# Attention with beacon keys and a multiplicative feed-forward: from stages set by a scheduler to one hand-ordered stream

## The chip, the core and the metric

The kernel runs on one core of one Trainium2 chip. The metric is device time in microseconds. Engines are TensorE (PE; its weight loads are PEld), VectorE (DVE), ScalarE (ACT), GpSimd (POOL) and SyncE (SP). Each has its own instruction queue and works through it in order; semaphores join them. DMAs are issued from the SP or the POOL queue.

## What is computed

```python
B, H, S, Nb, D = (8, 8, 576, 16, 64)          # tokens: B*S = 4608
k_all = np.concatenate([beacon_k, k], axis=2)  # 592 keys
v_all = np.concatenate([beacon_v, v], axis=2)
scores = np.matmul(q, k_all.transpose(0, 1, 3, 2)) / np.sqrt(D)
# causal on the 576 own keys; the 16 beacon keys are always seen
a = np.exp(scores - scores.max(-1, keepdims=True))
a /= a.sum(-1, keepdims=True) + 1e-09
x = np.matmul(a, v_all)                        # -> [4608, 512]
return ((x @ w1) * (x @ w2) @ w3) @ w_out      # d_model 512, d_ff 1024
```

Inputs and output are f32 in DRAM. Both kernels work in f16 with f32 sums in PSUM.

## The kernel before

It is written stage by stage, and a scheduler orders the instructions from their dependences and from the number of buffers of each pool.

*Weights* (L85 to L114): each is loaded in f32, cast on DVE, and w3 is written back to DRAM in f16 (`w3s`) and read through eight DMA transposes (`w3T`). 64 matmuls then form `Wt` = w3 @ w_out, so that feed-forward needs only `Wt`.

*A batch* (loop over 8): q, k and v tiles are loaded in f32 (L168, SP), cast on ACT (q, k) or POOL (v) at L170, and q and k are written to DRAM in f16 (`qs`, `ks`, L201 and L205, POOL queue). For each of the four head pairs `t`, two DMA transposes bring q and k back with the head dimension on partitions (`qpT`, `kpT`, L215 and L216).

*Attention of a head pair*: scores are computed keys by queries, key tile after key tile (5 of them), into one PSUM tile `Ps` (L233, L238), exponentiated by ACT into `pT` (L243), and the diagonal block is masked by DVE (L253). Then v is stationary and `pT` moves: `P1` gets values (L265), `PD` gets denominators by a second stream with a tile of ones as weights (L272). A reciprocal of the whole `PD` (L281) and a product (L282) give `xT`, already transposed for feed-forward.

*Feed-forward* (`moe_chunk`, 512 tokens): 64 matmuls into `pab` (L135), scaled by ACT (`a_sb`) and multiplied by DVE (`gT`), then 32 into `po` (L148), scaled by ACT (`ot`) and stored. `pab` and `po` use the PSUM banks of `P1`, `PD` and `Ps`, one buffer each, so attention and feed-forward take turns. Chunk b − 1 is written ahead of batch b's attention; the last two chunks stand behind everything.

Of the kernel before, what the change touches and what calls it, by code (L numbers as in the profile page):

```python
# [19 lines left out]
def kernel(  # L20
# [24 lines left out]
    HD = H * D  # L45

    SC = 5
# [1 line left out]
    KJ = [min(P, NJ - jt * P) for jt in range(NJT)]
    SLO = [max(0, P * jt - Nb) for jt in range(NJT)]  # L50
# [2 lines left out]
    dramp = ctx.enter_context(tc.tile_pool(name="dram", bufs=1, space=bass.MemoryType.DRAM))

    xT = const.tile([P, NKT, M], FP16)
    w12 = const.tile([P, NKT, 2 * DF], FP16)
    Wt = const.tile([P, NFT, DM], FP16)
    ones = const.tile([P, 64], FP16)
    nc.vector.memset(ones, 1.0)
    ebias = const.tile([P, 1], FP32)  # L60
    nc.vector.memset(ebias, EXP_BIAS)
    LT = const.tile([P, P], FP16)
    LT0 = const.tile([P, 112], FP16)
    nc.vector.memset(LT, 1.0)
    nc.vector.memset(LT0, 1.0)
    for m, base in ((LT, 0), (LT0, Nb)):
# [10 lines left out]
    qs = dramp.tile([B, SC * P, NT, P], FP16)  # L77
    ks = dramp.tile([B, NJT * P, NT, P], FP16)
    w3s = dramp.tile([DF, DF], FP16)

    with (
        tc.tile_pool(name="wst", bufs=1) as wst,
        tc.tile_pool(name="wpsum", bufs=2, space=bass.MemoryType.PSUM) as wpsum,
    ):
        w12_32 = wst.tile([P, NKT, DF], FP32)  # L85
        for i, w in enumerate((moe_w1, moe_w2)):
            nc.sync.dma_start(w12_32, w.rearrange("(t p) f -> p t f", p=P))
            nc.vector.tensor_copy(
                w12[:, :, ds(i * DF, DF)],
                w12_32,  # L90
            )
        wo32 = wst.tile([P, NFT, DM], FP32)
        wo16 = wst.tile([P, NFT, DM], FP16)
        nc.sync.dma_start(wo32, moe_w_out.rearrange("(t p) n -> p t n", p=P))
        nc.vector.tensor_copy(wo16, wo32)
        w3_32 = wst.tile([P, NFT, DF], FP32)
        w3h = wst.tile([P, NFT, DF], FP16)
        w3T = wst.tile([P, NFT, DF], FP16)
        nc.sync.dma_start(w3_32, moe_w3.rearrange("(t p) r -> p t r", p=P))
        nc.vector.tensor_copy(w3h, w3_32)  # L100
        nc.sync.dma_start(w3s.rearrange("(t p) r -> p t r", p=P), w3h)
        for rt in range(NFT):
            nc.sync.dma_start_transpose(w3T[:, rt, :], w3s[:, ts(rt, P)])  # L103
# [21 lines left out]
    scale = float(D**-0.5)

    def moe_chunk(mc):
        gT = mp.tile([P, NFT, 512], FP16, tag="gT", name="gT")
        for kf in range(NFT):
            pab = aps.tile(  # L130
                [P, 2, 512], FP32, tag="P1" if kf % 2 == 0 else "PD", name="pab"
            )
            for i in range(2):
                for kt in range(NKT):
                    nc.tensor.matmul(  # L135
                        pab[:, i, :],
                        w12[:, kt, ds(i * DF + kf * P, P)],
                        xT[:, kt, ds(mc * 512, 512)],
                        start=(kt == 0),
                        stop=(kt == NKT - 1),  # L140
                    )
            a_sb = mp.tile([P, 512], FP32, tag="a_sb", name="a_sb")
            nc.scalar.activation(a_sb, pab[:, 0, :], AF.Copy, scale=GS)  # L143
            nc.vector.tensor_tensor(gT[:, kf, :], pab[:, 1, :], a_sb, ALU.mult)  # L144
        po = aps.tile([P, 4, DM], FP32, tag="Ps", name="po")
        for mt in range(4):
            for kf in range(NFT):
                nc.tensor.matmul(  # L148
                    po[:, mt, :],
                    gT[:, kf, ts(mt, P)],  # L150
                    Wt[:, kf, :],
                    start=(kf == 0),
                    stop=(kf == NFT - 1),
                )
# [163 lines left out]
```

## Time and profile before

| | |
|---|---|
| median of 3 runs | 668.42 us (667.52 to 668.67) |
| span of the profiled execution | 666.6 us, 7292 instructions |
| TensorE busy | 425.0 us, 64% |
| DVE, ACT, POOL busy | 256.4, 243.0, 64.9 us |
| first feed-forward weight matmul, first score matmul | 45.75 us, 91.11 us |
| DMA | 72.58 MB, 109 GB/s on average |

Busy time is the time in which an engine had an instruction at work; matmuls are pipelined, so a busy TensorE is not a full one. The granted clock is the share of full speed that TensorE was given; its two levels are 1.2 and 2.4 GHz. The chain follows the work that ended last back from the end, at each step to what released it.

### The profile page before, as it was taken

What the parts mean: (1) busy time and instruction counts of PE and PEld (TensorE: products, weight loads), DVE (VectorE), ACT (ScalarE), POOL (GpSimd) and SP (SyncE); (2) the same over time, 40 slices, a digit from 0 to 9 for tenths busy, and PEclk for the clock granted to TensorE, in tenths of its full rate; (3) what the DMA queues carried; (4) which work ended last, traced back from release to release, by engine and by line L of the source; (5) the groups of instructions that cost most, each with busy time, mean ns of one, the idle gap of its engine ahead of it and who ended that gap; (6) DMA issues with size and microseconds to landing.
All of it is one profiled execution on the core that took longest, in us unless ns stands there. A gap on an engine that the chain in (4) does not pass through costs nothing.

```text
span 666.6 us, 7292 instructions
## 1 busy us (share of the span) xinstructions
PE 425.0 (64%) x2848; PEld 201.7 (30%) x2848; DVE 256.4 (38%) x464; ACT 243.0 (36%) x357; POOL 64.9 (10%) x114
## 2 busy tenths in 40 slices
PE   0019116677667865785678666966696759665994
PEld 0003003333323333333333233323333323333441
DVE  2300004741464146424642455235532553255320
ACT  0002416534653464345434431344234323442331
POOL 0000110203002110210021001000100000000001
PEclk9999755589556965796659655965697569765998
DMA  8772879595939756662266111021001000100011
GB/s 340 290 201 50 215 165 243 107 247 153 265 98 212 213 133 156 149 190 50 37 147 192 49 37 19 18 65 37 19 16 48 1 0 17 47 1 1 16 48 63
DMA packets 172723, 72.58 MB, mean 109 GB/s; under 512 B 163856, under 2 KB 163984, under 8 KB 172688
## 3 DMA queue, kind: packets, MB, share of 16 engines
q1 hardware_dynamic: 166864, 53.10, 33.9%
q0 software_dynamic: 5824, 19.01, 7.4%
q8 instruction: 22, 0.36, 0.2%
q14 instruction: 13, 0.11, 0.1%
HBM read 39.32 MB, written 21.10 MB: 91 GB/s over the span
## 4 chain that ended last, share of the span: by engine, by line
PE 55%; ACT 19%; DMA 9%; DVE 8%; SPq 4%; issue 3%; POOL 0%; POOLq 0%; ACTq 0%
PE pab L135 21%; ACT pT L243 15%; PE po L148 9%; PE Ps L233 9%; PE P L265 7%; DVE rdb L281 6%; PE PD L272 6%; DMA w<-in_moe_w_dram 4%; ACT ot L156 3%; PE pw L107 2%; DMA t_k<-in_k_dram 2%; PE Ps L238 2%; SPq L103 1%; SPq L216 1%; DMA w3s<-w3h 1%
## 5 line engine op out<-in xcount | busy, mean ns | idle before, releaser
L243 ACT ACTIVATE pT<-Ps,ebias 128x1152 f16<-128x1152 f32 (+4 forms) x160 | 130.2, 814 | 143.9 <-PE Ps L238 137.3
L233 PE MATMUL Ps<-qpT,kpT 64*128 64x512 f16 (+4 forms) x320 | 77.1, 378 | 135.9 <-ACT pT L243 107.7
L135 PE MATMUL pab<-xT,w 128*128 128x512 f16 x576 | 143.5, 413 | 31.2 <-DVE rdb L281 30.8
L281 DVE RECIPROCAL rdb<-PD 128x576 f16<-128x576 f32 x32 | 120.2, 3757 | 65.9 <-PE P L265 37.8
L253 DVE TENSOR_TENSOR pT<-pT,LT 128x128 f16<-128x128 f16 (+2 forms) x320 | 55.3, 216 | 199.5 <-ACT pT L243 199.5
L265 PE MATMUL P<-pT,v 128*64 128x64 f16 (+6 forms) x640 | 113.3, 333 | 1.5 <-DVE xT L282 0.9
L272 PE MATMUL PD<-pT,ones 128*64 128x64 f16 (+6 forms) x640 | 107.3, 330 | 0.2 <-DVE pT L253 0.2
L135 PEld LDWEIGHTS <-w 128*128 128x128 f16 x576 | 60.2, 104 | 110.5 <-issue 54.1
L144 DVE TENSOR_TENSOR gT<-pab,a_sb 128x512 f16<-128x512 f32 x72 | 49.8, 691 | 105.5 <-ACT a_sb L143 105.5
L143 ACT ACTIVATE a_sb<-pab 128x512 f32<-128x512 f32 x72 | 43.0, 597 | 109.6 <-PE pab L135 109.2
L148 PE MATMUL po<-Wt,gT 128*128 128x512 f16 x288 | 69.2, 379 | 16.7 <-ACT ot L156 16.4
L265 PEld LDWEIGHTS <-v 128*64 128x64 f16 (+1 forms) x640 | 59.7, 152 | 37.0 <-issue 28.8
L272 PEld LDWEIGHTS <-ones 128*64 128x64 f16 (+1 forms) x640 | 63.5, 156 | 8.5 <-issue 1.9
L238 PEld LDWEIGHTS <-kpT 64*128 64x128 f16 (+1 forms) x320 | 22.4, 117 | 132.3 <-issue 130.8
L107 PE MATMUL pw<-wo,w3T 128*128 128x512 f16 x64 | 20.7, 476 | 48.2 <-DMA w3T<-w3s 47.9
L238 PE MATMUL Ps<-qpT,kpT 64*128 64x64 f16 (+1 forms) x320 | 48.7, 245 | 0.0
L233 PEld LDWEIGHTS <-kpT 64*128 64x128 f16 (+1 forms) x320 | 31.1, 114 | 49.6 <-issue 44.6
L156 ACT ACTIVATE ot<-po 128x512 f32<-128x512 f32 x36 | 21.5, 597 | 63.4 <-PE po L148 63.4
L148 PEld LDWEIGHTS <-gT 128*128 128x128 f16 x288 | 27.4, 97 | 56.4 <-issue 23.2
L157 POOL DMA_DIRECT2D out_dram<-ot x36 | 19.5, 543 | 231.3 <-ACT ot L156 231.3
L170 POOL CAST v<-t_v 128x512 f16<-128x512 f32 (+1 forms) x40 | 23.2, 615 | 138.4 <-PE PD L272 135.5
L170 ACT CAST q<-t_q 128x512 f16<-128x512 f32 (+1 forms) x40 | 24.2, 612 | 31.2 <-DMA t_q<-in_q_dram 31.1
(21 smaller groups left out, 94.3 us busy)
## 6 DMA issues: line engine op xcount, KB each, us to landing
out_dram<-ot POOLq DMA_DIRECT2D x36, 256.0 KB, 2.3
t_q<-in_q_dram SPq DMA_DIRECT2D x32, 256.0 KB, 3.7
t_k<-in_k_dram SPq DMA_DIRECT2D x24, 256.0 KB, 4.1
t_v<-in_v_dram SPq DMA_DIRECT2D x24, 256.0 KB, 4.2
w<-in_moe_w_dram SPq DMA_DIRECT2D x2, 2048.0 KB, 8.5
w<-in_moe_w_dram SPq DMA_DIRECT2D x1, 4096.0 KB, 19.1
qs<-q POOLq DMA_DIRECT2D x8, 512.0 KB, 4.6
ks<-k POOLq DMA_DIRECT2D x8, 512.0 KB, 4.2
```

Of the source, the lines that this page charges most:

```text
L135: nc.tensor.matmul(pab[:, i, :], w12[:, kt, ds(i * DF + kf * P, P)], xT[:, kt, ds(mc * 512, 512)], start=(kt == 0), stop=(kt == NKT - 1),)
L143: nc.scalar.activation(a_sb, pab[:, 0, :], AF.Copy, scale=GS)
L144: nc.vector.tensor_tensor(gT[:, kf, :], pab[:, 1, :], a_sb, ALU.mult)
L148: nc.tensor.matmul(po[:, mt, :], gT[:, kf, ts(mt, P)], Wt[:, kf, :], start=(kf == 0), stop=(kf == NFT - 1),)
L170: (eng.copy if eng is nc.scalar else eng.tensor_copy)(d16[:n, c], t32[:n])
L233: nc.tensor.matmul(Ps[:kj, hh, ds(lo, 512 - lo)], lhs, qpT[ds(hh * 64, 64), ds(lo, 512 - lo)],)
L238: nc.tensor.matmul(Ps[:kj, hh, ds(512, 64)], lhs, qpT[ds(hh * 64, 64), ds(512, 64)],)
L243: nc.scalar.activation(pT[:kj, :, jt, ds(lo, S - lo)], Ps[:kj, :, ds(lo, S - lo)], AF.Exp, bias=ebias[:kj], scale=scale,)
L253: nc.vector.tensor_tensor(pT[:kj, hh, jt, ds(lo, w)], pT[:kj, hh, jt, ds(lo, w)], msk[:kj, :w], ALU.mult,)
L265: nc.tensor.matmul(P1[ds(64 * hh, 64), ds(s0, sn)], v16[:kj, jt, ds(hh * 64 + 128 * t, 64)], pT[:kj, hh, jt, ds(s0, sn)], start=first, sto ...
L272: nc.tensor.matmul(PD[ds(64 * (1 - hh), 64), ds(s0, sn)], ones[:kj, 0:64], pT[:kj, 1 - hh, jt, ds(s0, sn)], start=first, stop=last,)
L281: nc.vector.reciprocal(rdb, PD)
```

## The change

The kernel is written anew for the same computation.

- *Loads* go from f32 in DRAM to f16 in SBUF in one casting DMA each, issued by POOL; the casts on DVE, ACT and POOL, and the DRAM copies `qs`, `ks`, `w3s`, are gone. Batches 0 and 1 and all weights are queued at the start, in the order q/k of 0, v of 0, w1, w2, batch 1, w3, w_out.
- *Transposes* of q, k and w3 read SBUF and write SBUF. w3 lies for the time in the second half of `xT`.
- *Scores* of a head pair are cut into four groups of 368, 512, 384 and 400 columns for each head (`GROUPS`, with `GO` their places in `pT`). `ps` has two buffers of two banks. The heads alternate matmul by matmul. There is one exponential a group, and one mask multiply for groups 0, 2 and 3.
- *Values*: a 128 x 128 block of probabilities is stationary, and 65 columns of `va` move: 64 of v and one of ones, so the denominator is column 64 of the same result (`BLK`, `DONE`). Queries now lie on partitions: the reciprocal is of 2 or 4 numbers a partition, and the product writes `x16`, [queries, 512].
- `x16` needs a transpose: for the last head pair of a batch five more DMA transposes write `xT`.
- *Feed-forward* has three PSUM banks of its own (`psM`) and is a Python generator that gives one matmul at a time. The output is scaled by DVE and stored from SP.
- *Order*: manual. Step s issues the scores of s + 2, some feed-forward matmuls, the mask of s + 1 and the values of s. There are 8 x 4 x 4 = 128 steps; feed-forward begins at step 20, and 696 of its 928 matmuls (with the 64 of `Wt`) lie between steps. Loads of batch b + 1 are issued in steps 0 to 4 of batch b, its transposes in steps 4 to 8.

```diff
+GROUPS = [
+    [(1, 112, 128, 0), (0, 0, 240, 128)],
+    [(0, 240, 256, 0), (1, 240, 256, 256)],
+    [(3, 368, 128, 0), (2, 240, 256, 128)],
+    [(4, 496, 80, 0), (3, 496, 80, 80), (2, 496, 80, 160), (1, 496, 80, 240), (0, 496, 80, 320)],
+]
+GW = [368, 512, 384, 400]
+BLK = [
+    [(0, GO[0] + 128)],
+    [(0, GO[0] + 240), (1, GO[0])],
+    [(0, GO[1]), (1, GO[1] + 256), (2, GO[2] + 128)],
+    [(0, GO[1] + 128), (1, GO[1] + 384), (2, GO[2] + 256), (3, GO[2])],
+    [(4, 0), (3, 80), (2, 160), (1, 240), (0, 320)],
+]
+DONE = [[0, 1], [], [2, 3], [4]]
...
+    psS = ctx.enter_context(tc.tile_pool(name="psS", bufs=2, space=bass.MemoryType.PSUM))
+    psV = ctx.enter_context(tc.tile_pool(name="psV", bufs=1, space=bass.MemoryType.PSUM))
+    psM = ctx.enter_context(tc.tile_pool(name="psM", bufs=3, space=bass.MemoryType.PSUM))
+    ctx.enter_context(tc.manual_schedule())
...
+    def load_q(b, c):
+        rows = min(P, S - c * P)
+        nc.gpsimd.dma_start(
+            q16s[b % NB2][:rows, c, :].rearrange("s (h d) -> s h d", h=H),
+            q[b, :, ds(c * P, rows), :].rearrange("h s d -> s h d"),
+        )
...
+    def transpose_qk(b, c):
+        i = b % NB2
+        rows = min(P, S - c * P)
+        nc.sync.dma_start_transpose(qTs[i][:, :, ds(c * P, rows)], q16s[i][:rows, c, :])
+        nc.sync.dma_start_transpose(kTs[i][:, :, ds(c * P, P)], k16s[i][:, c, :])
...
+    def scores(s):
...
+        for jt, q0, n, col in GROUPS[g]:
+            for hh in range(2):
+                nc.tensor.matmul(
+                    ps[:, hh, ds(col, n)],
+                    kT[ds(hh * 64, 64), t, ts(jt, P)],
+                    qT[ds(hh * 64, 64), t, ds(q0, n)],
+                )
+        nc.scalar.activation(
+            pT[:, :, ds(GO[g], GW[g])], ps[:, :, 0 : GW[g]], AF.Exp, scale=scale
+        )
...
+    def values(s):
...
+        for n, i in enumerate(tiles):
+            for hh in range(2):
+                for jn, (jt, col) in enumerate(BLK[i]):
                     nc.tensor.matmul(
+                        pv[:, 2 * n + hh, 0:65],
+                        pT[:, hh, ds(col, P)],
+                        va[:, jt, 2 * t + hh, 0:65],
+                        start=(jn == 0),
+                        stop=(jn == len(BLK[i]) - 1),
                     )
+        nc.vector.reciprocal(rd[:, 0 : 2 * ni], pv[:, 0 : 2 * ni, 64])
...
+        if t == NT - 1:
+            for i in tiles:
+                nc.sync.dma_start_transpose(
+                    xT[:, :, ds(b * S + QT0[i], QTN[i])], x16[: QTN[i], i, :]
                 )
...
+    S0 = 20
+    FF_END = 7 * 96 + 64 - 40
+    scores(0)
+    scores(1)
+    mask(0)
+    for s in range(NS):
+        b, r = s // 16, s % 16
+        if s + 2 < NS:
+            scores(s + 2)
+        if s >= S0:
+            emit_ff((FF_END * (s - S0 + 1)) // (NS - S0))
+        if s + 1 < NS:
+            mask(s + 1)
+        values(s)
+        if 1 <= b < B - 1:
+            if r < NJT:
+                load_q(b + 1, r)
+                load_k(b + 1, r)
+                load_v(b + 1, r)
+            if 4 <= r < 4 + NJT:
+                transpose_qk(b + 1, r - 4)
+    emit_ff(1 << 30)
```

How this moves instructions shows on ACT and TensorE. On ACT before, in the attention of batch 1 (`q` and `t_q` are the next batch's f16 and f32 tiles):

```order
L243 ACTIVATE pT<-Ps,ebias 128x2x336
L170 CAST q_1686<-t_q_0_1689 128x512
L243 ACTIVATE pT<-Ps,ebias 128x2x208
L243 ACTIVATE pT<-Ps,ebias 80x2x80
L170 CAST q_1686<-t_q_1_1692 128x512
L170 CAST q_1686<-t_q_2_1695 128x512
L243 ACTIVATE pT<-Ps,ebias 128x2x576
```

On ACT now, in batch 1 where feed-forward begins (`pm` is a feed-forward bank, `ps` a score buffer):

```order
L275 ACTIVATE pT<-ps 128x2x384
L198 ACTIVATE a_sb<-pm 128x512
L275 ACTIVATE pT<-ps 128x2x400
L198 ACTIVATE a_sb<-pm 128x512
L275 ACTIVATE pT<-ps 128x2x368
L275 ACTIVATE pT<-ps 128x2x512
```

The casts between the exponentials, each behind a DMA, are replaced by scaled copies of feed-forward results.

On TensorE before, between two head pairs (`P`, `PD` are values and denominators):

```order
L265 LDWEIGHTS v_608
L265 MATMUL P_902<-pT,v_608 64x64
L272 LDWEIGHTS ones
L272 MATMUL PD<-pT,ones 64x64
L238 LDWEIGHTS kpT
L238 MATMUL Ps<-qpT,kpT 128x64
L233 LDWEIGHTS kpT
L233 MATMUL Ps<-qpT,kpT 128x512
```

On TensorE now, in one step in the middle (`w` the feed-forward weights, `pv` values and denominators):

```order
L270 LDWEIGHTS kT_72
L270 MATMUL ps<-qT_70,kT_72 128x256
L187 LDWEIGHTS w_59
L187 MATMUL pm<-xT,w_59 128x512
...
L208 LDWEIGHTS gT
L208 MATMUL pm<-Wt,gT 128x512
L306 LDWEIGHTS pT
L306 MATMUL pv<-va_68,pT 128x65
```

Between the scores of a later step and the values of this one stand six or seven feed-forward matmuls.

## Rows read from the trace of the kernel before

**Rows 1.** The page, part 1: busy us (share of the span), instructions, by engine.

```profile
PE 425.0 (64%) x2848; PEld 201.7 (30%) x2848; DVE 256.4 (38%) x464; ACT 243.0 (36%) x357; POOL 64.9 (10%) x114
```

**Rows 2.** The page, part 2: tenths in 40 slices, TensorE busy and granted clock.

```profile
PE   0019116677667865785678666966696759665994
...
PEclk9999755589556965796659655965697569765998
```

**Rows 3.** The page, part 4: the chain that ended last, by engine.

```profile
PE 55%; ACT 19%; DMA 9%; DVE 8%; SPq 4%; issue 3%; POOL 0%; POOLq 0%; ACTq 0%
```

**Rows 4.** Windows: start:end length, each engine's busy us (instructions), clock, DMA share, GB/s.

```profile
240.00:260.00 20.00, 12.17 (x119) 6.37 (x115) 11.70 (x23) 10.65 (x15) 1.86 (x3) 0.50 0.79 189
...
637.80:649.00 11.20, 11.20 (x54) 5.04 (x53) 4.14 (x6) 4.18 (x7) 0.54 (x1) 1.00 0.08 31
```

**Rows 5.** Timeline: start us, length us, instruction, count, [idle before, releaser].

```profile
91.11 0.61 PE L233 MATMUL Ps<-qpT,kpT 64*128 64x512 f16 x2 [22.24 <-DMA kpT<-ks]
...
93.15 0.52 PE L233 MATMUL Ps<-qpT,kpT 64*128 64x400 f16 x2 [1.37 <-ACT pT L243]
...
93.76 1.03 ACT L243 ACTIVATE pT<-Ps,ebias 128x928 f16<-128x928 f32 x1 [0.66 <-PE Ps L238]
...
105.90 3.76 DVE L281 RECIPROCAL rdb<-PD 128x576 f16<-128x576 f32 x1 [2.04 <-PE P L265]
...
612.00 16.36 PE L135 MATMUL pab<-xT,w 128*128 128x512 f16 x64 [3.85 <-DVE rdb L281]
```

**Rows 6.** Timeline, TensorE in the tail: a half-clock weight load, a full-clock run.

```profile
613.67 0.15 PEld L135 LDWEIGHTS <-w 128*128 128x128 f16 x1 [0.28 <-issue]
...
637.77 11.39 PE L135 MATMUL pab<-xT,w 128*128 128x512 f16 x52
```

**Rows 7.** Groups by line and shape: count, busy us, mean ns, idle before, releaser.

```profile
L144 DVE TENSOR_TENSOR gT<-pab,a_sb 128x512 f16<-128x512 f32 x72 | 49.8, 691 | 105.5 <-ACT a_sb L143 105.5
...
L281 DVE RECIPROCAL rdb<-PD 128x576 f16<-128x576 f32 x32 | 120.2, 3757 | 65.9 <-PE P L265 37.8 <-PE PD L272 28.2
L143 ACT ACTIVATE a_sb<-pab 128x512 f32<-128x512 f32 x72 | 43.0, 597 | 109.6 <-PE pab L135 109.2
L243 ACT ACTIVATE pT<-Ps,ebias 128x1152 f16<-128x1152 f32 x32 | 39.1, 1221 | 79.8 <-PE Ps L238 73.4 <-issue 6.4
...
L148 PEld LDWEIGHTS <-gT 128*128 128x128 f16 x288 | 27.4, 97 | 56.4 <-issue 23.2 <-DVE gT L144 4.0
L282 DVE TENSOR_TENSOR xT<-P,rdb 128x576 f16<-128x576 f32 x32 | 24.2, 757 | 0.3
L243 ACT ACTIVATE pT<-Ps,ebias 128x416 f16<-128x416 f32 x32 | 19.4, 607 | 11.7 <-PE Ps L238 11.7
L233 PE MATMUL Ps<-qpT,kpT 64*128 64x400 f16 x64 | 15.3, 457 | 43.0 <-ACT pT L243 43.0
```

**Rows 8.** Groups by line: DMA issues on POOL, of 128 runs and of 512.

```profile
L157 POOL DMA_DIRECT2D out_dram<-ot x36 | 19.5, 543 | 231.3 <-ACT ot L156 231.3
...
L201 POOL DMA_DIRECT2D qs<-q x8 | 6.5, 807 | 148.6 <-DMA t_k<-in_k_dram 74.5 <-ACT q L170 74.1
```

**Rows 9.** Timeline of SP's queue: one of the 64 q and k transposes.

```profile
93.20 1.26 SPq L216 DMA_TRANSPOSE kpT<-ks  x1
```

**Rows 10.** Windows: weights loading; w3's transposes; q, k and v loading.

```profile
1.00:30.00 29.00, 0.00 (x0) 0.00 (x0) 7.15 (x6) 1.09 (x1) 0.52 (x2) 1.00 0.92 362
...
45.50:55.00 9.50, 7.06 (x14) 0.92 (x14) 0.00 (x0) 0.00 (x0) 0.00 (x0) 1.00 0.99 179
...
76.00:84.00 8.00, 0.00 (x0) 0.00 (x0) 0.00 (x0) 3.50 (x6) 3.44 (x6) 0.50 1.12 288
```

**Rows 11.** DMA issues: count, KB each, median us from issue to landing.

```profile
t_q<-in_q_dram SPq DMA_DIRECT2D x32, 256.0 KB, 3.7
...
qpT<-qs SPq DMA_TRANSPOSE x32, 2.8
```

**Rows 12.** Timeline, ACT: the last output copy.

```profile
658.72 0.60 ACT L156 ACTIVATE ot<-po 128x512 f32<-128x512 f32 x1 [1.98 <-PE po L148]
```

More of the change, by code (lines that the diff above doesn't have):

```diff
@@ L44 @@
     NFT = DF // P
[L45 to L47 removed]
     NJT = 5
[L49 to L50 removed]
+    NB2 = 2
+    VS = 72
+    scale = float(D**-0.5)
     const = ctx.enter_context(tc.tile_pool(name="const", bufs=1))
[L53 to L66, printed above, removed]
+    xT = const.tile([P, NKT, M], FP16, name="xT")
+    w12 = const.tile([P, NKT, 2 * DF], FP16, name="w12")
+    Wt = const.tile([P, NFT, DM], FP16, name="Wt")
+    wo16 = const.tile([P, NFT, DM], FP16, name="wo16")
@@ L75 @@
         )
[L77 to L103, printed above, removed]
@@ new lines, with ff_ab @@
+    nc.gpsimd.dma_start(wo16, moe_w_out.rearrange("(t p) n -> p t n", p=P))
+    for kt in range(NFT):
+        nc.sync.dma_start_transpose(w3T[:, :, ts(kt, P)], w316[:, kt // 2, kt % 2])
+    def ff_ab(mc):
+        gT = gp.tile([P, NFT, 512], FP16, name="gT")
+        for kf in range(NFT):
+            a_sb = None
+            for i in range(2):
+                pm = psM.tile([P, 512], FP32, name="pm")
+                for kt in range(NKT):
+                    nc.tensor.matmul(
+                        pm,
+                        w12[:, kt, ds(i * DF + kf * P, P)],
+                        xT[:, kt, ds(mc * 512, 512)],
+                        start=(kt == 0),
+                        stop=(kt == NKT - 1),
+                    )
+                    if kt < NKT - 1:
+                        yield
+                if i == 0:
+                    a_sb = asb.tile([P, 512], FP32, name="a_sb")
+                    nc.scalar.activation(a_sb, pm, AF.Copy, scale=GS)
+                else:
+                    nc.vector.tensor_tensor(gT[:, kf, :], pm, a_sb, ALU.mult)
+                yield
+        return gT
@@ new lines, in ff_out @@
+    def ff_out(mc, gT):
+        for mt in range(4):
+            pm = psM.tile([P, 512], FP32, name="pm")
+            for kf in range(NFT):
+                nc.tensor.matmul(
+                    pm,
+                    gT[:, kf, ts(mt, P)],
+                    Wt[:, kf, :],
+                    start=(kf == 0),
+                    stop=(kf == NFT - 1),
+                )
+                if kf < NFT - 1:
+                    yield
+            ot = op.tile([P, DM], FP32, name="ot")
+            nc.vector.tensor_scalar(ot, pm, float(1.0 / GS), None, ALU.mult)
+            nc.sync.dma_start(out[ds(mc * 512 + mt * P, P), :], ot)
+            yield
@@ L125 @@
[L125 to L134, printed above, removed]
-                    nc.tensor.matmul(
[L136 to L140, printed above, removed]
-                    )
[L142 to L153, printed above, removed]
-                )
-            ot = op.tile([P, DM], FP32, tag="ot", name="ot")
-            nc.scalar.activation(ot, po[:, mt, :], AF.Copy, scale=float(1.0 / GS))
-            nc.gpsimd.dma_start(out[ds(mc * 512 + mt * P, P), :], ot)
@@ L284, with stream, emit_ff @@
-    for mc in (B - 1, B):
-        moe_chunk(mc)
-    actx.close()
+                if rt < NFT - 1:
+                    yield
+            nc.scalar.copy(Wt[:, kt, :], pm)
+            yield
+    def stream():
+        for mc in range(M // 512):
+            gT = yield from ff_ab(mc)
+            if mc == 0:
+                yield from fuse()
+            yield from ff_out(mc, gT)
+    ff = stream()
+    emitted = 0
+    def emit_ff(upto):
+        nonlocal emitted
+        while emitted < upto:
+            try:
+                next(ff)
+            except StopIteration:
+                return
+            emitted += 1
```

243 lines of the change are left out of this document (111 added, 132 removed).

## The prediction

> **What bounds the kernel now.** I read the busy shares first: no engine is above 64% of the 666.6 us span [rows 1], so nothing is saturated and the time lies in hand-offs. The slices show when: TensorE is busy six to eight tenths almost everywhere, and its granted clock falls to 0.5 in the attention stretches and rises again in the feed-forward ones [rows 2]. The chain that ended last is 55% TensorE with ACT, DVE and DMA behind it [rows 3]. Two stretches show why [rows 4]: in attention (240 to 260 us) TensorE works 12.17 of 20 us at 0.50 (1.2 GHz), in feed-forward (637.8 to 649) 11.20 of 11.20 at 1.00 (2.4 GHz). In the attention stretch one PSUM tile `Ps` is filled, exponentiated and filled again: a score matmul sat 1.37 us behind the exponential, the next exponential 0.66 us behind the scores; then the 3.76 us reciprocal sits between the last `PD` and whoever wants that bank next, and the first tail matmul stood 3.85 us behind one [rows 5]. Scores begin only at 91 us [rows 5], because every weight is loaded, cast and transposed first. From there to 612 us is 521 us for eight batches, 65 each; the two closing chunks are the rest.
>
> **Feed-forward: 928 matmuls, as before.** 576 + 288 + 64 of 512 columns. At the full clock 52 of them took 11.39 us, 0.219 each with its weight load hidden [rows 6]: 203 us. At the half clock the pitch is 0.15 + 0.28 = 0.43 [rows 6]. The change can alter where they lie and at which clock, not their number.
>
> **Scores.** Per head pair 1664 columns for each head, in 11 pairs (128, 240, three of 256, another 128, five of 80). Heads use different row halves, and two 400-column matmuls together took 0.52 us where one takes 0.457 [rows 5, 7]: a pair costs as one. At 0.428 ns a column the 1008 columns of the wide pairs are 0.43 us; the seven narrow pairs I put at 0.07 for their weight loads: 0.92 us per head pair, 29 us in all. Ends: 23 (columns alone) and 59 (no overlap of heads).
>
> **Values.** The 1280 matmuls with v and ones become 960 of 65 columns (15 query-by-key blocks, two heads, 32 head pairs), each with its own 128-column load of probabilities. No row shows that form. Lower end: 128 columns at 0.428 ns, 0.055 us, if the load alone paces. Upper end: a whole load of 0.097 [rows 7] and then 65 columns, 0.125. I take 0.07, near the lower end, since the 0.219 pitch shows loads hidden entirely: 67 us (53 to 120). The Trainium skill (TensorE: Matmul & The Clock Gate, Back-to-back issue gap) gives about 81 ns for a sustained load-and-matmul stream of 128 columns; by that estimate the forecast would be 9 us longer, and no run so far shows it.
>
> **ACT** loses the casts, the output copies and one exponential in five. From the exponentials of 1152 and 416 elements [rows 7], 0.834 ns an element and 0.26 fixed: four of 736 to 1024 elements make 3.82 us a head pair, 0.95 a step (a step is one of the four score groups; there are 128).
>
> **DVE** loses the 32 long reciprocals: 3757 ns for 576 is 6.5 ns an element [rows 7], so four denominators cost some 0.13 us with a fixed part. The multiply from PSUM (757 at 576, 691 at 512 [rows 7]) gives 0.43 for 256 elements and 0.30 for 128. Masks at the same 1.03 ns an element are the dear end: 1.48 us a head pair. Together 0.76 us a step.
>
> **A step with feed-forward.** From step 20 on 696 feed-forward matmuls are spread over 108 steps, 6.44 each: 1.41 us, with 0.53 of values and 0.23 of scores 2.17 us of TensorE at the full clock. ACT has 0.95 plus 63 copies of 0.597 [rows 7] over the 108 steps, 1.30. DVE has 0.76 plus 55 products and 24 output scalings, 1.26. So TensorE is last, and the exponential that it waited for is now two steps old. The single `pv` bank must be read before the next values: reciprocal and multiply, 0.56 us, behind 1.6 us of scores and feed-forward. Because TensorE never waits for long I expect the full clock: 108 × 2.17 = 234 us, plus 12 that I allow for hand-offs (5%) and 2 for the half clock at its start.
>
> **Queues that must keep up in 16 steps, 35 us.** POOL now casts on load: 17 DMAs a batch. An issue takes 0.543 with 128 runs and 0.807 with 512 [rows 8], hence 1.16 with 1024, 20 us. SP: 15 transposes at 1.26 [rows 9] and four or five stores, 21 us. DMA engines: 3.6 MB of loads at 288 GB/s, 1.9 MB of transposes at 179, 1.2 MB of stores at the weights' 362 [rows 10], 12.5 + 10.6 + 3.3 = 26 us. All fit, none by much.
>
> **The head.** POOL set-up 2 us; the fifth load issued at about 6, landed 3.7 later, its transpose 2.8 after that [rows 11]: first scores at 13 us, not 91. Batch 0 has no feed-forward and runs at the half clock, 2 × (0.92 + 2.1) = 6 us a head pair, 24 us. But batch 1 queues behind w1 and w2: 12.5 + 11.6 us for loads and weights, 7.3 for transposes (1.3 MB), 3.6 for its own first four loads (1.05 MB), from 5 us on, gives 40, and 44 with transposes; the stream waits for it in step 14. Its v lands by 50 and four more steps end at 52. There feed-forward begins. w3 and w_out follow (6.3 MB, 17 us), just before step 30 (74 us) wants them, and batch 2's first pieces come some 7 us too late for the scores two steps ahead; I charge those 7.
>
> **The tail.** 928 − 696 = 232 matmuls, 51 us dense at the full clock. The end after the last output copy began was 666.6 − 658.72 = 7.9 us [rows 12]; 8 again.
>
> **Sum.** 52 + 234 + 12 + 2 + 7 + 51 + 8 = 366 us of span; the shown median lies 1.8 above the profiled span: **368 us**.
>
> **Rivals.**
> *DMA paces (18%).* The casting loads write 128-byte runs. Should a batch's loads take twice 12.5 us, the queues need 39 us a batch: 6 × 4 more, and 36 in the head for three batches, 428 us; at three times, near 540. For it: loads of 256-byte runs reach 288 GB/s where the weights reach 362 [rows 10]. Against: that loss is small, and reads do not shrink. The Trainium skill (DMA: Bandwidth & Descriptors, Specifications) says that below 512 bytes the engine reads, modifies and writes; the direction agrees with those two rows, the size isn't given.
> *The clock stays at the half level (8%).* Then a step is 4.3 us, 108 of them 468, and the total about 600. For it: attention matmuls ran at 0.50 while 61% busy. Against: any dense run of 512-column matmuls reached 1.00 [rows 4], and they are two thirds of every step.
> *Slower than before (3%), by one mechanism.* No row shows a transpose that reads SBUF. SP runs them in order, 15 a batch. If one held the queue for X, a batch takes 15 X; 668 us in all means 76 us a batch, so it decides from X = 5.1 us. At X = 2.8, each landing before the next goes, it is 42 us a batch, about 430 (5%). Against: 1.26 us an issue, 179 GB/s while they ran alone [rows 9, 10].
> *It doesn't interleave.* The stream is written by hand, so the order holds; but a late gT or a_sb would stall values behind it in TensorE's queue. That is inside the 12 us.
>
> **How the numbers follow.** The forecast with its bounds, 335 (0.055 for values, no hand-offs, no late batch 2) to 415 (0.125 for values), has 64%; below it 2%; DMA 18%, of which half ends by 450; half clock 8%; slow transposes 8%; so 335 to 450 holds about 8 in 10. Faster 0.96, within 0.2% (about what this kernel's measurement can tell from no change) 0.01, slower 0.03.
>
> **What would show it.** Right: first scores near 13 us; granted clock at 1.0 from about 55 us to the end; 65-column matmuls 0.055 to 0.08 apart; a batch every 35 to 38 us; the last 51 us pure feed-forward. Wrong: a DMA share near 1 with TensorE waiting on `qT`, `kT` or `va` at batch starts; transposes over 2 us apart on SP; TensorE waiting on `pv`'s readers; slices of 0.5 in the middle. The largest lever is the 2.17: each tenth of a us per step is 11 us.

## The result

| | before | after |
|---|---|---|
| median | 668.1 us | 379.2 us (376.8 to 382.9, 4 runs) |
| span of the profiled execution | 666.6 us | 378.2 us (time 379.9) |
| TensorE busy | 425.0 us, 64% | 289.4 us, 77% |
| first score matmul | 91.11 us | 18.50 us |
| first feed-forward matmul on tokens | 139.56 us | 106.37 us |

The ratio is 0.567, with a 95% interval of 0.564 to 0.569. The forecast was 368 (335 to 450). One run of the changed kernel and two of e9 below fell in a slower state of the chip; the ratio and the comparisons leave them out.

The page of the changed kernel, part 2 (tenths of each of 40 slices, 9.5 us each), against [rows 2]:

```profile
PE   0016620300079999999999999999999999999995
PEclk9999999999999999999999999999999999999999
DMA  9999999999990299989959999998995120420302
```

Two things stand in these lines. From the 13th slice to the last but one TensorE's digits are 9, with the granted clock at 9 as well, where [rows 2] have mostly six to eight tenths and a clock that falls to 5 again and again. In the 9th to 11th slice TensorE does nothing while the DMA row reads 9. So the middle went as forecast, or better, and the start did not. TensorE's waits, by what ended them (total us, times, longest; `x` in the rows is `x16`):

```profile
PE ps L270 <- DMA kT<-k: 40.3, 6, 18.5
PE pm L187 <- DMA xT<-x: 36.0, 1, 36.0
PE ps L270 <- DMA qT<-q: 7.2, 2, 4.1
PE pv L306 <- DVE x L315: 1.2, 7, 0.2
```

TensorE's waits for ACT and DVE of [rows 5], 1.37 and 3.85 us, have no successor but the 1.2 us in the last line: all others are for transposes, and they lie in the first 107 us. (ACT still waits for scores, which costs nothing while TensorE is last.) One head pair in the middle (TensorE's timeline: start, length, instruction, count):

```profile
199.79 0.33 PE L270 MATMUL ps<-qT,kT 64*128 64x128 f16 x4
...
201.36 0.59 PE L306 MATMUL pv<-va,pT 128*128 128x65 f16 x14
201.88 0.39 PE L270 MATMUL ps<-qT,kT 64*128 64x256 f16 x4
...
203.72 0.47 PE L306 MATMUL pv<-va,pT 128*128 128x65 f16 x10
204.12 0.34 PE L270 MATMUL ps<-qT,kT 64*128 64x128 f16 x4
...
207.88 0.33 PE L270 MATMUL ps<-qT,kT 64*128 64x128 f16 x4
```

From one first score group to the next it is 8.09 us, four steps of 2.02. The values are 14, 10 and (at 205.70) 6 matmuls; from their start to that of the next instruction they take 0.52, 0.40 and 0.28 us, 0.040 each. The four score groups, read the same way, take 0.26, 0.32, 0.28 and 0.28. The rest is feed-forward. Windows (start:end, length, busy us of PE, PEld, DVE, ACT, POOL with counts, clock, DMA share, GB/s):

```profile
160.00:200.00 40.00, 40.00 (x389) 20.25 (x387) 22.49 (x61) 23.70 (x32) 17.21 (x22) 1.00 1.31 136
280.00:320.00 40.00, 40.00 (x389) 20.27 (x388) 22.90 (x61) 23.81 (x33) 0.00 (x0) 1.00 0.28 70
```

TensorE works all 40 us at 1.00, where the attention stretch of [rows 4] had 12.17 of 20 us at 0.50; DVE and ACT stand near half. With 1.31 of DMA share or 0.28, it gets through the same 389 instructions, so the DMA does not pace the middle.

By stages of the forecast, in us:

| stage | forecast | profiled execution |
|---|---|---|
| to the first feed-forward matmul | 52 | 106.4 |
| 108 steps (234 + 12 + 2 + 7) | 255 | 217.6 (to 323.99) |
| 232 closing matmuls | 51 | 50.2 |
| end | 8 | 4.0 |
| span | 366 | 378.2 |

The total came out 12 us off because +54 at the start and −37 in the steps nearly cancel. The experiments take up both.

### The profile page after: what moved, and what is told of

Same layout as the page of the kernel before. It is cut to its first block, busy times and chain, and to the rows that moved or that the text cites. A ratio compares the mean times of both kernels' runs of the same rounds, so it can differ in the third digit from the quotient of the medians.

```text
span 378.2 us, 6634 instructions
## 1 busy us (share of the span) xinstructions
PE 289.4 (77%) x2592; PEld 145.5 (38%) x2592; DVE 153.1 (40%) x410; ACT 155.6 (41%) x209; POOL 115.9 (31%) x153
## 4 chain that ended last, share of the span: by engine, by line
PE 71%; DMA 21%; POOL 3%; SPq 3%; issue 1%; DVE 0%; POOLq 0%
PE pm L187 35%; PE pm L208 17%; PE ps L270 8%; PE pv L306 7%; DMA k<-in_k_dram 6%; DMA xT<-in_moe_w_dram 6%; DMA w<-in_moe_w_dram 5%; PE pm L226 4%; DMA va<-in_v_dram 3%; DMA xT<-x 2%; POOL q L126 2%; SPq L326 2%; SPq L177 1%; POOL k L135 1%; DVE ot L218 0%
## 5 line engine op out<-in xcount | busy, mean ns | idle before, releaser
L187 PE MATMUL pm<-xT,w 128*128 128x512 f16 x576 | 138.7, 383 | 36.0 <-DMA xT<-x 36.0
L275 ACT ACTIVATE pT<-ps 128x736 f16<-128x736 f32 (+3 forms) x128 | 110.1, 864 | 126.0 <-PE ps L270 124.3
L270 PE MATMUL ps<-qT,kT 64*128 64x80 f16 (+3 forms) x704 | 48.7, 247 | 47.5 <-DMA kT<-k 40.3
L198 ACT ACTIVATE a_sb<-pm 128x512 f32<-128x512 f32 x72 | 42.9, 596 | 83.3 <-PE pm L187 81.4
L200 DVE TENSOR_TENSOR gT<-pm,a_sb 128x512 f16<-128x512 f32 x72 | 49.8, 692 | 60.9 <-PE pm L187 42.5
L208 PE MATMUL pm<-Wt,gT 128*128 128x512 f16 x288 | 68.7, 380 | 0.0
L306 PEld LDWEIGHTS <-pT 128*128 128x128 f16 x960 | 44.4, 103 | 26.7 <-DVE x L315 4.9
L306 PE MATMUL pv<-va,pT 128*128 128x65 f16 x960 | 49.3, 201 | 1.3 <-DVE x L315 1.2
L126 POOL DMA_DIRECT2D q<-in_q_dram x40 | 35.1, 877 | 13.2 <-DMA w<-in_moe_w_dram 4.0
L315 DVE TENSOR_TENSOR x<-pv,rd 128x256 f16<-128x256 f32 (+1 forms) x96 | 36.5, 380 | 3.4
L208 PEld LDWEIGHTS <-gT 128*128 128x128 f16 x288 | 25.7, 98 | 31.4 <-issue 3.5
L226 PE MATMUL pm<-wo,w3T 128*128 128x512 f16 x64 | 15.6, 381 | 0.0
## 6 DMA issues: line engine op xcount, KB each, us to landing
xT<-in_moe_w_dram POOLq DMA_DIRECT2D x4, 512.0 KB, 18.7
```

The lines of the kernel that those rows point to most:

```text
L126: nc.gpsimd.dma_start(q16s[b % NB2][:rows, c, :].rearrange("s (h d) -> s h d", h=H), q[b, :, ds(c * P, rows), :].rearrange("h s d -> s h d"),)
L187: nc.tensor.matmul(pm, w12[:, kt, ds(i * DF + kf * P, P)], xT[:, kt, ds(mc * 512, 512)], start=(kt == 0), stop=(kt == NKT - 1),)
L198: nc.scalar.activation(a_sb, pm, AF.Copy, scale=GS)
L200: nc.vector.tensor_tensor(gT[:, kf, :], pm, a_sb, ALU.mult)
L208: nc.tensor.matmul(pm, gT[:, kf, ts(mt, P)], Wt[:, kf, :], start=(kf == 0), stop=(kf == NFT - 1),)
L226: nc.tensor.matmul(pm, w3T[:, rt, ts(kt, P)], wo16[:, rt, :], start=(rt == 0), stop=(rt == NFT - 1),)
```

## Experiments on the start

My theory after the two traces: feed-forward's 36 us wait for `xT` is a place in SP's queue. SP, changed kernel:

```profile
62.70 30.27 SPq L177 DMA_TRANSPOSE w3T<-xT  x8
93.06 7.29 SPq L326 DMA_TRANSPOSE xT<-x  x5
```

The five `x16` transposes of batch 0 stand behind w3's eight, which wait for w3's casting loads (18.7 us from issue to landing) though the fuse needs them later. The rival: the DMA engines are simply full.

**e1, w3's transposes behind those of batch 0.**

```diff
-    for kt in range(NFT):
-        nc.sync.dma_start_transpose(w3T[:, :, ts(kt, P)], w316[:, kt // 2, kt % 2])
...
+        if s == 15:
+            for kt in range(NFT):
+                nc.sync.dma_start_transpose(w3T[:, :, ts(kt, P)], w316[:, kt // 2, kt % 2])
```

> The changed kernel with one edit: the eight transposes of w3 stand on SP's queue behind the xT transposes of batch 0 (issued after step 15) instead of ahead of them. In the changed kernel feed-forward began at 106.4 us after a wait of 36.0 us for xT, whose transposes SP issued at 93.1, behind w3's (62.7 to 93.0). Theory A (SP's order costs it): first feed-forward matmul at 70 to 75 us; the fuse of w3 and w_out ten steps later still finds w3T nearly ready and batch 2's scores wait 5 to 15 us; median 348 to 362 us. Rival B (the loads themselves are late, so the wait only changes its name): feed-forward begins early, but the 30 us come back as waits for w3T and for batch 2's q and k, median 370 to 382.

Measured 365.95 us (364.67 to 366.56), between the two ranges: 13.3 less than the changed kernel. TensorE, and SP under it:

```profile
82.54 2.72 PE L184 MATMUL pm<-xT,w 128*128 128x512 f16 x6 [10.71 <-DMA xT<-x]
...
111.40 0.49 PE L267 MATMUL ps<-qT,kT 64*128 64x128 f16 x4 [7.74 <-DMA kT<-k]
```
```profile
52.73 20.87 SPq L323 DMA_TRANSPOSE xT<-x  x5
73.69 27.45 SPq L350 DMA_TRANSPOSE w3T<-xT  x8
```

Feed-forward starts 24 us earlier. Yet the five transposes took 21 us on SP, where they had taken 7.29, w3's eight 27, and batch 2's, now behind those, let TensorE wait 7.74 us. The queue place is real and worth 13 us of the 54. Of the 36.0 us, 10.7 are left as the wait for `xT`, 8.2 came back in the waits for `kT` (48.5 us in all), and TensorE's own busy time grew by 2.6.

**m1, what the DMAs cost by themselves.** One run of a kernel of loads and transposes alone.

> No attention and no feed-forward, the output is zeros: only DMAs, in four stages one after the other. Casting loads of three batches from POOL; plain f32 loads of three batches from SP; forty transposes SBUF to SBUF of 128 x 512; then casting loads of two batches beside forty transposes. The prediction: 12.5 us a batch for loads of either kind, 1.26 us a transpose. Theory A (casting loads run at half the speed): 22 to 28 us a batch against 13 to 15 for plain ones; transposes 1.2 to 1.4 us apart. Rival B (casting costs nothing, the late landings in the head come from queueing alone): 13 to 16 us a batch for both. In the last stage, if loads and transposes share the engines fairly: 25 us of loads and 10 of transposes a batch, some 70 us together; if not, less.

VectorE's timeline in it, where it waits for the last casting and the last plain load:

```profile
43.96 0.36 DVE L130 CAST q<-q 128x320 f32<-128x320 f16 x1 [41.38 <-DMA q<-in_q_dram]
...
99.09 0.35 DVE L139 CAST q<-v 64x320 f16<-64x320 f32 x1 [0.28 <-DMA v<-in_v_dram]
```

Three batches of casting loads were in at 43.96 us, 14.2 a batch from 1.25 on; three batches of plain f32 loads, issued from 46.40 us, at 99.09, 17.6 a batch. So a batch of casting loads into 128-byte runs is not later than a plain one. Windows of the two stages (busy us of DVE and POOL, clock, DMA share, GB/s) show that this does not price the DMA engines:

```profile
5.00:40.00 35.00, 0.00 (x0) 35.00 (x44) 1.00 2.06 131
50.00:95.00 45.00, 1.05 (x3) 0.00 (x0) 1.00 1.34 215
```

POOL was issuing in all of the 35 us, so the 14.2 us are the pace of its 17 issues a batch, and the DMA share is higher with casting. The Trainium skill (DMA: Bandwidth & Descriptors, Specifications) has a read-modify-write below 512 bytes; runs of 128 and of 256 bytes both lie below that, so m1 does not show what it costs. Forty transposes went out in 53 us, mostly 1.31 apart. DMA issues of this kernel (KB each, median us from issue to landing), and of the changed one:

```profile
q<-in_q_dram POOLq DMA_DIRECT2D x20, 128.0 KB, 4.4
qT<-q SPq DMA_TRANSPOSE x40, 2.5
```
```profile
q<-in_q_dram POOLq DMA_DIRECT2D x32, 128.0 KB, 7.6
qT<-q SPq DMA_TRANSPOSE x40, 6.8
```

With queues full of other work a casting load takes 7.6 us instead of 4.4 to land, a transpose 6.8 instead of 2.5. By an estimate at these prices, with 2 us of set-up, the two batches and w1, w2 ahead of feed-forward (28 us, 4.2 MB at 10.6 MB in 42.7 us, so 17, and 20 transposes of 1.31, 26) are 47 us if transposes hide and 73 if not. TensorE got batch 1's last `kT` at 66.8.

**e5, another order of the start.** Batch 1 is loaded ahead of w1 and w2, w3 and w_out behind batch 2 (at step 20); two first halves come ahead of the fuse.

```diff
+        g0 = yield from ff_ab(0)
+        g1 = yield from ff_ab(1)
+        yield from fuse()
...
-    S0 = 20
+    S0, S1 = 22, 34
...
+        if s == 20:
...
+        if 32 <= s < 32 + NFT:
+            kt = s - 32
+            nc.sync.dma_start_transpose(w3T[:, :, ts(kt, P)], w316[:, kt // 2, kt % 2])
```

> Only the order of the start is changed against the changed kernel: batch 1 is queued before w1 and w2; w3 and w_out are loaded behind batch 2's tiles (step 20) and w3's transposes go out one a step in steps 32 to 39; the second chunk's first half comes before the fuse, and feed-forward begins at step 22 with 64 matmuls until step 34. Theory A, the long start is a matter of queue order: nothing waits behind what is needed later, feed-forward's first matmul is at 60 to 72 us, TensorE's waits for kT or xT after it stay under 4 us each, and the time is 345 to 358 us. Theory B, the start is bounded by the data rate (17 to 20 MB at some 215 GB/s are wanted by then in any order): what is won at one place comes back at another, and the time is that of e1, 360 to 370 us.

359.95 us (357.86 to 361.81), 0.538 of before (0.535 to 0.540) and the fastest kernel here, at the lower edge of theory B. Feed-forward begins at 70.00 us, but the waits only spread out, the last of them 4.42 us for `xT` until 108.26:

```profile
70.00 2.29 PE L179 MATMUL pm<-xT,w 128*128 128x512 f16 x5 [5.22 <-DMA xT<-x]
...
108.26 2.72 PE L179 MATMUL pm<-xT,w 128*128 128x512 f16 x6 [4.42 <-DMA xT<-x]
```

**e6, gates.** Two elements of `kT` are copied on POOL ahead of the loads of w1 and w2, and again ahead of w3's, so that these loads aren't queued before the transposes have landed; w3's stand at step 24 instead of 20.

```diff
+    nc.gpsimd.tensor_copy(gate, kTs[1][:, 0, 4 * P : 4 * P + 2])
     for i, w in enumerate((moe_w1, moe_w2)):
```

> The kernel of e5 (359.95 us) with two gates in POOL's queue: a copy of two elements of kT, which waits until batch 1's last transpose has landed, stands ahead of the loads of w1 and w2, and one that waits for batch 2's last transpose ahead of the loads of w3 and w_out. In e5 the last kT of batch 1 was issued at 41.1 us and TensorE had it at 59.8. Theory A, transposes already issued are held up by the casting loads that were queued meanwhile: with the gates they land 2 to 5 us after issue, the waits for kT in batch 1 (9.2 and 4.1 us) and batch 2 shrink by half or more, and the time falls by 4 to 12 us, to 348 to 356. Theory B, the sum of all bytes paces the start whatever goes first: TensorE waits for xT or w instead, and the time stays within 3 us of 360 or rises.

361.87 us (360.26 to 363.83): no gain. But look where TensorE waits; in e5 it was 39.0 us for `kT`, 9.8 for `qT` and 9.6 for `xT`. In e6:

```profile
PE ps L267 <- DMA kT<-k: 22.3, 5, 18.4
PE ps L267 <- DMA qT<-q: 16.4, 4, 9.2
PE pm L181 <- DMA xT<-x: 13.2, 1, 13.2
PE pm L181 <- DMA w<-in_moe_w_dram: 8.2, 2, 5.2
```

Theory A's mechanism is there: with nothing queued against them the transposes land sooner, and the waits for `kT` fall from 39.0 to 22.3 us. Theory B's total is there too: the weights are now late by 8.2, `qT` by 6.6 more and `xT` by 3.6. In these runs what goes first decides which tile is late, not how long the start is. That it must be so isn't shown: the two gates also held POOL's whole queue, for 12.2 and 13.1 us.

**e7 and e9, w3 later still.** e7 loads w3 at step 36 and fuses behind the third chunk's first half; e9 also moves w3's transposes from steps 44 to 51 to 48 to 55, behind batch 2's `x16`. Both also have a third `gT` buffer and one fewer of `a_sb` and `ot`.

```diff
+        g2 = yield from ff_ab(2)
         yield from fuse()
...
-        if 32 <= s < 32 + NFT:
+        if 44 <= s < 44 + NFT:
```

> The kernel of e5 (359.95 us) with w3 and w_out loaded 16 steps later (step 36, transposes in steps 44 to 51), and the fuse behind the third chunk's first half instead of the second's; feed-forward is thinner until step 48 (128 matmuls) and denser after it. Theory A, e5's waits around step 30 (3.2, 3.1, 1.9 for batch 2's tiles and 4.4 for xT, between 87 and 108 us) come from w3's 6 MB in front of or beside them: they go, and the time is 346 to 354 us. Theory B, the DMA engines are full until the last batch is loaded, so the 6 MB only move the gap: batch 3 or 4 is late instead, and the time is 357 to 365 us.

> The kernel of e7 (374.5 us) with w3's eight transposes in steps 48 to 55 instead of 44 to 51, so that none stands in SP's queue ahead of an x16 transpose of batch 2 (steps 44 to 47). In e7 TensorE waited 19.5 us for xT at 143 us, with w3's transposes between those of x16 on SP. Theory A, the wait is that queue place again, as in the changed kernel: it falls under 6 us, nothing else grows by more than 3, and the time is 354 to 362 us, level with e5. Theory B, x16's transposes are late because the DMA engines are full of w3, w_out and batch 4: a wait of 12 us or more stays at the third chunk and the time is 368 to 375 us.

e7 took 374.54 us (373.56 to 375.68), worse than either theory said. Batch 2's tiles are hardly late any more (a wait of 0.6 us; 3.1 for `xT` behind it and 3.3 for batch 3), but one wait for `xT`, until 142.96 us, costs 19.54. SP in e7:

```profile
116.63 8.62 SPq L323 DMA_TRANSPOSE xT<-x  x2
125.34 8.43 SPq L362 DMA_TRANSPOSE w3T<-xT  x2
133.86 3.24 SPq L323 DMA_TRANSPOSE xT<-x  x2
```

Two of w3's transposes stand between those of `x16`: the changed kernel's fault again, this time of my own making. e9 took 363.5 and 365.5 us, and the wait stays:

```profile
134.74 1.86 PE L179 MATMUL pm<-xT,w 128*128 128x512 f16 x4 [14.84 <-DMA xT<-x]
```

By e9's theories the wait decides for B: of 19.5 us the queue place was 4.7. In the rest SP needs 15.6 us for five `x16` transposes (7.29 in the changed kernel) while w3, w_out and batch 4 are loading; that the DMA engines' rate is the reason is likely, but no run separates it. The time lies between A's range and B's, and the rest of e9's gain on e7 isn't traced to one wait.

## Experiments on the step

**e8, one step of lead instead of two.**

```diff
-        if s + 2 < NS:
-            scores(s + 2)
+        if s + 1 < NS:
+            scores(s + 1)
...
-        if s + 1 < NS:
-            mask(s + 1)
+        mask(s)
```

> The changed kernel (379 us) with scores issued one step ahead of their values instead of two, and the mask in the step of its values. Theory A, feed-forward between the groups alone hides the exponential and the mask (1.4 us of it lie between scores and values in each step, and exponential plus mask take 1.2 to 1.4 us): in feed-forward's steps nothing changes, the four steps a head pair of batch 0 lose at most 1 us each where the start waits for data anyway, and the time is 377 to 384 us. Theory B, the second step of lead is what keeps TensorE from waiting: 0.3 to 1 us a step at 108 steps, 410 us or more, with waits of the values for VectorE's mask.

424.45 us (422.08 to 425.06): theory B, 45 us dearer. TensorE's waits for the mask, 37.0 us where the changed kernel has none, and one of them on DVE and TensorE:

```profile
PE pv L306 <- DVE pT L287: 37.0, 52, 1.3
```
```profile
223.62 1.47 PE L208 MATMUL pm<-Wt,gT 128*128 128x512 f16 x6
...
225.13 0.69 DVE L218 TENSOR_SCALAR ot<-pm 128x512 f32<-128x512 f32 x1 [1.28 <-DMA kT<-k]
...
225.74 0.42 DVE L287 TENSOR_TENSOR pT<-pT,MB 128x512 f16<-128x512 f16 x1
...
226.30 0.52 PE L306 MATMUL pv<-va,pT 128*128 128x65 f16 x12 [1.15 <-DVE pT L287]
```

The exponential was done at 222.64 (221.83 + 0.81), yet the values wait 1.15 us until 226.30: their mask stands on DVE behind an output scaling, which could not start before its own matmuls ended at 225.09 (223.62 + 1.47). My sum of exponential and mask had left out DVE's in-order queue. Two steps of lead with the mask a step ahead cover it (the edit takes back both, and no run separates them); this is the part of the design that makes the 12 us of hand-offs in my forecast zero.

**e2, feed-forward in lumps after each batch.**

```diff
-        if s >= S0:
+        if s >= S0 and s % 16 == 15:
```

> The changed kernel, but the 696 feed-forward matmuls are issued in lumps after the last step of each batch instead of 6.44 a step. Theory A (interleaving hides exponentials and keeps the clock up): an attention head pair alone takes 4.48 us as in batch 0 of the changed kernel, 27 of them 121 us, at the half clock, and the lumps 696 x 0.216 = 150 plus 2 to 3 us at 0.43 each: 280 us where the changed kernel takes 213, total 435 to 460. Rival B (TensorE's work is the same in any order and buffers hide the rest): within 10 us of 379.

468.38 us in the one run made, 89 more and 8 above theory A's range. Waits, and a stretch of attention at a batch's start (busy us of PE, PEld, DVE, ACT, POOL, then as above):

```profile
PE ps L270 <- DMA kT<-k: 83.7, 12, 27.7
```
```profile
190.00:200.00 10.00, 4.88 (x64) 3.13 (x64) 3.42 (x12) 4.41 (x6) 4.36 (x6) 0.50 2.00 155
```

Against the changed kernel the waits for `kT`, `qT` and `x16` grow by 43, 22 (to 28.8) and 16 us and that for `xT` (36) goes, +45 together. The other half is TensorE's own busy time, 331.7 us against 289.4, with attention at the granted clock of 0.50, as in [rows 4]. Between groups, feed-forward hides the waits, keeps the clock up, and spreads the loads over the batch. The rival falls.

**e4, v and ones stationary again.** e1 with the old form of the values: 60 matmuls of up to 128 queries a head pair, the reciprocal on 128 partitions, no `x16`.

```diff
-                        pv[:, 2 * n + hh, 0:65],
-                        pT[:, hh, ds(col, P)],
-                        va[:, jt, 2 * t + hh, 0:65],
+                            pv[ds(hh * 64, 64), d, n, 0:w],
+                            va[:, jt, 2 * t + hh, 0:64] if d == 0 else ones[:, jt // 4, :],
+                            pT[:, hh, ds(col, w)],
```

> The kernel of run e1 (w3's transposes late, 366 us) with one part of the change undone: v and a tile of ones are stationary again, 64 columns each, the probabilities move in blocks of up to 128 queries, the reciprocal is of all 576 denominators of a head pair on 128 partitions, and the product writes xT itself, so that the x16 transposes are gone. Theory A, the form of the values is worth little inside the stream, since TensorE stays last: 30 side-by-side pairs of 128 columns cost 0.054 each against 30 matmuls at 0.040, 0.4 us a head pair or 11 us in all, and the 10.7 us wait for xT goes: 362 to 372 us. Theory B, the reciprocal turns into the new wait: at 6.5 ns an element 256 denominators take 1.7 us and with the product 2.1 us, longer than the 1.7 us of scores and feed-forward that lie between two uses of the one pv bank, and VectorE needs 7.8 of some 8.4 us: TensorE then shows waits behind L305's neighbours on VectorE in every head pair, 1 us or more each: 385 to 410 us.

397.99 us (397.9 to 402.41), 32 above e1 and in theory B's range. The pages' busy rows, e1 first, and in e4 the waits and one reciprocal:

```profile
PE 292.0 (80%) x2592; PEld 146.4 (40%) x2592; DVE 153.2 (42%) x410; ACT 155.7 (43%) x209; POOL 115.9 (32%) x153
PE 324.8 (82%) x3552; PEld 159.6 (40%) x3552; DVE 266.2 (67%) x477; ACT 155.8 (39%) x209; POOL 116.0 (29%) x153
```
```profile
PE pv L306 <- DVE xT L321: 32.5, 40, 1.9
...
205.97 1.76 DVE L320 RECIPROCAL rd<-pv 128x256 f32<-128x256 f32 x1
```

The 1.76 us reciprocal of 256 denominators, 6.9 ns each against the 6.5 of [rows 7], holds the single `pv` bank, and values wait 32.5 us in all; the changed kernel's takes 0.18. That these are just the 32 us is a coincidence. 18.3 of the 32.5 lie ahead of feed-forward (until 74.83 us), and e4 waits less for transposes: 35.1 us (31.4 for `kT`, 3.7 for `qT`) where e1 has 67.3 (48.5, 8.1, and 10.7 for `xT`). Waits cancel, and what is left is TensorE's own work: 3552 matmuls instead of 2592, 324.8 us instead of 292.0. So the new form of the values is worth about 32 us inside this stream, although `x16` has to be transposed for it, and by its fewer matmuls no less than by the short reciprocal. A second `pv` bank wasn't tried.

**e3, heads apart.** One head's score matmuls first, then the other's.

```diff
-        for jt, q0, n, col in GROUPS[g]:
-            for hh in range(2):
+        for hh in range(2):
+            for jt, q0, n, col in GROUPS[g]:
```

> The changed kernel, but the score matmuls of a group are issued first all of one head, then all of the other, instead of alternating. Theory A (the two row halves run side by side only when neighbours in the queue): scores of a head pair go from 1.14 us to about 2.0, 27 head pairs 23 us, median 395 to 405. Rival B (a matmul of the other row half starts as soon as its rows are free, whatever stands between): within 4 us of 379.

379.32 us (378.19 to 383.3), no change: ten 80-column matmuls take 0.33 us instead of 0.28, and the rest is as it was. Four of 256 take 0.33, where m3 below makes it 0.45 on one row half alone, so the two heads run side by side in either order.

**m2 and m3, TensorE's prices.** One run each: stretches of short matmuls, each with a new weight tile, between stretches of 512 columns. In m2 each matmul has a PSUM tile of its own; in m3 several share one, as in the kernel.

> TensorE alone: 48 matmuls of 512 columns, then seven stretches of 64 matmuls, each with another 128-column weight tile than the one before it, between stretches of 16 of 512 columns: 33, 65 and 128 columns on 128 rows; 80 columns with the two row halves in turn, 80 on one half only; 256 columns likewise. Nothing of the reference is computed and the output is zeros. Theory A, the weight load sets a floor: 33 and 65 columns both come at 0.036 to 0.042 us each, and 128 columns at 0.055. Theory B, the moving columns pace and loads are hidden: 33 columns come at 0.014 to 0.025, 65 at 0.028 to 0.04, 128 at 0.055. For the heads: if row halves run side by side, 256 columns in turn take 0.055 to 0.07 a matmul and 0.107 or more on one half only; 80 columns in turn 0.020 to 0.045 against 0.036 to 0.08.

> The stretches of m2 again (33, 65, 128 columns on 128 rows; 80 columns with the row halves in turn and on one half only; 256 columns likewise; 60 matmuls each, another weight tile than the one before, 16 matmuls of 512 columns between), but with 4 to 15 matmuls into one PSUM tile, as the kernel has them, where m2 gave each matmul a tile of its own. Nothing of the reference is computed and the output is zeros. Theory A, m2's floor of 0.058 to 0.063 us came from the tile of its own (bookkeeping at every matmul): 65 columns now come at 0.037 to 0.042 as in the changed kernel, 33 at 0.030 to 0.042, 80 in turn at 0.026 to 0.035. Theory B, the floor belongs to a matmul with a new weight tile: 0.058 or more again, and the kernel's 0.040 has another reason (its sums over key tiles).

TensorE, m2 first (64 of 65 columns), then m3 (60 of 33, 65 and 128; 80 with row halves in turn and on one half; 256 likewise; two of the stretches of 16 of 512 columns between them):

```profile
23.03 4.11 PE L95 MATMUL pm<-mv,wt 128*128 128x65 f16 x64
```
```profile
14.97 1.65 PE L92 MATMUL pm<-mv,wt 128*128 128x33 f16 x60
16.47 3.62 PE L86 MATMUL pm<-mv,wt 128*128 128x512 f16 x16
19.93 2.15 PE L97 MATMUL pm<-mv,wt 128*128 128x65 f16 x60
...
25.37 3.51 PE L102 MATMUL pm<-mv,wt 128*128 128x128 f16 x60
28.72 3.62 PE L86 MATMUL pm<-mv,wt 128*128 128x512 f16 x16
32.27 1.75 PE L108 MATMUL pp<-mv,wt 64*128 64x80 f16 x60
...
37.52 2.32 PE L115 MATMUL pp<-mv,wt 64*128 64x80 f16 x60
...
43.34 3.55 PE L121 MATMUL pp<-mv,wt 64*128 64x256 f16 x60
...
50.38 6.72 PE L128 MATMUL pp<-mv,wt 64*128 64x256 f16 x60
```

Length by count, a few ns too much for the end of the last, m2's 65 columns are 4.11 / 64 = 0.064 us each and m3's 2.15 / 60 = 0.036: the first is outside both of m2's theories. m2's floor goes with a PSUM tile of its own for every matmul, as m3's theory A has it; that the wait for an earlier matmul is the reason was not tested apart. In m3, 33 columns take 0.028 and 128 take 0.059, near the 0.055 of their columns at 0.428 ns. So a load costs at most 0.028, and behind 128 columns it is hidden. Row halves in turn nearly double the rate of wide scores (256 columns: 0.059 against 0.112 a matmul), but 80 columns only go from 0.039 to 0.029: a narrow pair is 0.058, where I had 0.07. The Trainium skill (TensorE: Matmul & The Clock Gate, Back-to-back issue gap) gives about 81 ns for a load-and-matmul stream of 128 columns; the 0.059 measured here is well under that.

The same lines show a price that nobody had asked for. The 16 matmuls of 512 columns take 3.46 us up to the next stretch when that one uses 128 rows (16.47 to 19.93), and 3.55 when it uses 64 (28.72 to 32.27): about 0.10 us for the change.

## Why the prediction held, and where it didn't

- *What bounded the old kernel*: right. Waits for hand-offs and the half clock are gone from the middle, and e2 brings both back.
- *Feed-forward*, 0.219 a matmul: right; 64 + 32 in the tail take 20.7 us, 0.216 each.
- *Values*, 0.07: too dear. 0.040 in the kernel, below my lower bound of 0.055. That bound took a whole 128-column load as the pace; m3's 33-column row shows that a load costs at most 0.028. Per head pair 1.20 us, not 2.1. The groups of 6, 10 and 14 grow by 0.12 us for every four, so each matmul adds 0.030, and some 0.10 a group does not depend on their number.
- *Scores*, 0.92 a head pair: 1.14. The two pairs of 256 take 0.32 where m3's 0.059 a matmul would make 0.24, and each of the four groups takes 0.10 to 0.12 us more than its 368, 512, 384 or 400 columns at 0.428 ns. That is the size of m3's change between 128 and 64 rows, which stands before and behind every score group. By this estimate the changes are 8 × 0.10 of a head pair's 8.09 us; the forecast had no such term, and no run tried fewer groups.
- *A step*, 2.17: these two make it 2.00 and the trace says 2.02, or 16 us of the 37. The 12 us of hand-offs, nil, and batch 2's 7 us, hidden by the longer start, are most of the rest.
- *ACT and DVE off the path*: right. Their terms held (exponentials 3.45 us a head pair against 3.82, products 0.42 and 0.29, long reciprocals gone). By the two rows named the masks' dear end is 1.68 us a head pair and not 1.48; they took 1.05.
- *The clock*: right, though full from some 110 us on and not from 55. What runs ahead of feed-forward is at the half clock: ten values in 0.73 us at 33.78 us against 0.47 at 203.72. The PEclk digits read 9 there, so here the durations had to tell it.
- *The start*, 52 us: this is the step that failed, at three places. First scores at 18.50, not 13: the transpose landed in some 7 us, not the 2.8 of [rows 11]. Batch 1's last tile at 66.8, not 44: I had put casting loads at 288 to 362 GB/s [rows 10], where m1 has 249 at POOL's pace, and let transposes hide. And 36 us for `xT`: I held w3's transposes against the fuse at step 30 alone, and did not ask what stood behind them on SP. e1 shows that place to be worth 13 us; e5 gets 19 by order; e6, e9 and the late landings point to the DMA engines' rate for most of the rest, but no run isolates it.
- *DMA paces* (a rival at 18%): not in the middle, as forecast, but as it seems in the start. Its price for casting, twice 12.5 us a batch, was not reached: 14.2 in m1, with POOL's issues (0.87 us, where I had 1.16) as the limit.
- *The tail and the end*: 50.2 and 4.0 against 51 and 8.
- *The signs set beforehand*: the last 51 us came as said. First scores, the start of the full clock, the 0.055 to 0.08 of the values and the 35 to 38 us a batch (16 steps of 2.02 are 32) did not, and transposes over 2 us apart, a sign of being wrong, were there in the start (w3's eight in 30.27 us).

The time lay inside the range because a start 54 us too short met steps 37 us too dear. The sign and the mechanism were right; the closeness was luck.

## What to carry to other kernels

For every transfer that a change puts into an in-order queue, ask not only when its own reader needs it but what stands behind it, and price the start by all bytes that must pass before each milestone, with transposes and loads competing. Matmuls that need nothing from the current step are best placed between dependent groups, with enough lead for the slowest in-order engine on the way, not just for the sum of the instructions. Count also how often neighbours in TensorE's queue change between 64 and 128 rows; it is 0.10 us each time here. When a forecast comes out right, compare it stage by stage: two errors of opposite sign look the same as none.
